# Moving the w_in operations of VectorE into the steps that form the bits, and GpSimd's split of the next pair's q ahead of its k

## The chip, the cores and the metric

One core of one Trainium2 chip runs the whole program. The metric is the device time of one execution in microseconds (us), median over the runs. The engines are called here as the profile calls them: PE (TensorE), DVE (VectorE), ACT (ScalarE), POOL (GpSimd) and SP (SyncE, which only issues DMAs here); PEld is the loading of PE's weights.

## What is computed

The reference is an attention whose mask comes from a hash, and then two feed-forward layers:

```python
def _attn_ref(q, k, v, proj):
    q_bits = (np.einsum('bhsd,dk->bhsk', q, proj) > 0).astype(np.int64)
    k_bits = (np.einsum('bhsd,dk->bhsk', k, proj) > 0).astype(np.int64)
    q_bucket, k_bucket = (np.sum(x * 2 ** np.arange(6), axis=-1) for x in (q_bits, k_bits))
    mask = q_bucket[:, :, :, None] == k_bucket[:, :, None, :]
    scores = np.where(mask, scale * np.matmul(q, k.transpose(0, 1, 3, 2)), -1e9)
    attn = np.exp(scores - np.max(scores, axis=-1, keepdims=True))
    attn = attn / (np.sum(attn, axis=-1, keepdims=True) + 1e-09)
    return np.matmul(attn, v)
def _moe_ref(x, w_in, w_out):
    h = np.maximum(x @ w_in, 0.0)
    return h * h @ w_out
def _moe2_ref(x, w_in, w_out):
    h = x @ w_in
    return h * (1.0 / (1.0 + np.exp(-h))) @ w_out
```

There are 2 batches of 8 heads, 768 positions of 64 dimensions; the layers take 1536 rows of 512 and widen them to 2048. All is float32; the kernel forms its products from two parts, a rounded high one and the rest.

## The kernel before

The 16 heads form eight pairs, p = 0 to 7. A pair is four units u (a head and one half of its 768 query rows), and a unit is three score tiles of 128 query rows by 768 keys. One loop, `for d in range(-5, ...)`, writes out the instructions of attention by hand: pass d, called **step d** here, issues on each engine a fixed list, and since each engine runs its queue in order, this order is the schedule. A step takes

- on DVE: the negated row maximum of the score tile of the step before (L983, `row_max`), the low part `tl` of the odd transposed block of the step before (L1023, `t_lo`), two tiny operations on the maximum (L987 and L988), then whatever the list `mid[d]` holds, then `tl` of the even block of this step;
- on PE: the transposes of two blocks of the probabilities (L1012, three matmuls each) into tiles `t`, the products with v of two earlier blocks (L1036 with the high part `th`, L1037 with `tl`), and the next score tile `s` (L976, four matmuls);
- on ACT: `th`, the rounded copy of each block (L1017), and the exponential of the score tile (L996);
- on POOL and SP: what the list `todo[d]` holds, at the end of the step.

The tiles `t` share three PSUM buffers in turn, so a block's transposes wait until the block three places earlier has been read by its `t_lo`.

In **a bits step** (d = 1, 10, 22, 34, 46, 58 and 70, the table `long`) PE also forms the hash products of a coming pair, eight matmuls with 32 columns of weights each, into a tile `bs` that takes one of the three buffers as well (L786, `bits_mm`). DVE therefore does the odd block's `t_lo` in the bits step already, right behind the even one, and in the next step compares `bs` with zero (L791, `bits_cmp`). ACT scales the pair's q after the hash products (L758).

In **a turn step** (d = 17, 29, 41, 53, 65, 77 and 88, the table `turn`) PE makes one more small transpose (L1251) and ACT copies its result.

The weights arrive as 64-bit floats in two 32-bit words, and the first layers' tiles are turned to float32 during attention. The table `W_STEPS` (line 41) holds for each of the four first w_in tiles the steps of its load, of |x| on ACT with the limits on POOL (L937, L941), and of three operations on DVE, which stand in `mid`: `w_exp` (L945, shifts), `w_sign` (L949) and `w_low` (L953), each on 128 x 512 words in SBUF. The last two read two SBUF tiles. `wp_put` (L960, L961, POOL) then rounds and splits the finished tile, for the first two.

Per pair POOL also rounds k and q (`cast_pair`, L754) into `hk` and `hq`, subtracts (`split_pair`, L774) into `lp`, splits v (`split_v`, L919 and L920), sums the outputs (`x_sum`, L1082) and starts one DMA per head for the high part of k (L764). For the second pair on, with d0 = 12(p - 1) and the bits step at d0 - 2, q and k are loaded by SP at d0 - 10 and d0 - 9, split around the bits step, and go to the score operands `qq` and `kk` by SP's DMAs: `hq` (L766), `lp` (L779 and L780, `place_lo`) and the bits (L909, `place_bits`). The first scores of the pair are issued at step d0 + 7.

Behind attention the two layers run by an order that a planner makes from costs at build time; the change doesn't touch it.

Of the kernel before, what the change touches and what calls it, by code (L numbers as in the profile page):

```python
# [37 lines left out]
W_LO = float(np.uint32(897 << 20).view(np.float32))  # L38
W_HI = float(np.uint32((1150 << 20) | 0xFFFFF).view(np.float32))
V_LAG = 4  # L40
W_STEPS = ((0, 5, 17, 29, 53), (8, 17, 41, 65, 77), (22, 29, 41, 92, 93), (54, 65, 92, 96, 96))
WA = 4
FB = 4
NP = FB // 2
# [655 lines left out]
def lsh_attention_moe_moe(ctx, tc, kd, qk, qf, fq, v, pc, wi1, wo1, wi2, wo2, out):  # L700
# [408 lines left out]
    def at(g, fn, *a):  # L1109
        todo[g].append((fn, a))  # L1110

    for p in range(1, NPAIR):
        d0 = 12 * (p - 1)
        if p > 1:
            at(d0 - 10, load_pair, p)
            at(d0 - 9, load_k, p)
            at(d0 - 4, new_hi, p)
            at(d0 - 4, cast_pair, p, 1)
            at(d0 - 3, split_pair, p, 1)
            scale[d0 - 2] = p  # L1120
            at(d0 - 2, cast_pair, p, 0)
            at(d0 - 1, split_pair, p, 0)
        else:
            at(0, split_pair, p, 0)
            at(0, split_pair, p, 1)
        long[max(d0 - 2, 1)] = p
        at(d0 + 1, load_head, p, 0)
        at(d0 + 2, place_lo, p, 0)
        at(d0 + 2, place_bits, p, 0)
        at(d0 + 5, load_v, p)  # L1130
        at(d0 + 8, split_v, p)
        at(d0 + 7, load_head, p, 1)
        at(d0 + 8, place_lo, p, 1)
        at(d0 + 8, place_bits, p, 1)
    for p in range(NPAIR):
        d0 = 12 * (p + 1)
# [12 lines left out]
    for k, d in enumerate(X_STEPS):  # L1149
        at(d, x_form, k)  # L1150
    for i, (d_load, d_abs, *d_dve) in enumerate(W_STEPS):
        key = (0, 0, i)
        at(d_load, w_load, key)
        at(d_abs, w_abs, key)
        at(d_abs, w_limit, key)
        for d, fn in zip(d_dve, (w_exp, w_sign, w_low)):
            mid[d].append((fn, (key,)))
        d0 = d_dve[2]
        if i < 2:
            at(d0, wp_put, i)  # L1160
    early = [(0, 1, i) for i in range(WB)]
    for i, key in enumerate(early):
        at(82 + 12 * i, w_load, key)
# [1 line left out]
    with tc.manual_schedule():  # L1165
# [106 lines left out]
        p = NPAIR - 1  # L1272
# [73 lines left out]
```

## Time and profile before

| what | value |
|---|---|
| time, median of 3 runs | 715.39 us (715.32 to 716.03) |
| the profiled execution's own time | 717.23 us |
| its span, first to last instruction | 715.5 us |
| busy: PE, DVE, ACT, POOL | 707.4 (99%), 605.4 (85%), 537.7 (75%), 257.6 us (36%) |
| DVE in the first thirteen of 40 slices | 90% or more in nearly all |
| granted TensorE clock | full (1.000 as a mean, the 2.4 GHz level) |

The profile is of one execution. Its times count from the first instruction; a row of the order of time gives the start, the duration, the engine, the line of the program, the operation with what it writes and reads, and in brackets how long the engine sat idle before it and what it waited for. Instructions on one engine overlap: the next may start some 0.1 us before the end that is shown for the one ahead. Attention takes the first 223 us or so, the two layers the rest.

### The profile page before, as it was taken

The numbers are of one execution on the slowest core, as the hardware profiler recorded it, in microseconds if no ns is written. First come the engines' busy times: TensorE is split into PE (matmuls) and PEld (weight loads), VectorE is DVE, ScalarE is ACT, GpSimd is POOL, SyncE is SP. The second block draws the span as 40 slices with busy tenths as digits, with TensorE's granted clock in tenths as the row PEclk, the third lists the DMA queues.
The fourth block names the chain that finished last, engine by engine and source line by source line (L and its number), as shares of the span: only waits on it lengthen the run. The fifth ranks groups of instructions, "written<-read, shape, count | busy, mean of one in ns | idle before, by whom it ended". The sixth has DMA issues, their size and how long they took to land.

```text
span 715.5 us, 10860 instructions
## 1 busy us (share of the span) xinstructions
PE 707.4 (99%) x3610; PEld 602.9 (84%) x3610; DVE 605.4 (85%) x1099; ACT 537.7 (75%) x1012; POOL 257.6 (36%) x239
## 2 busy tenths in 40 slices
PE   9999999999999999999999999999999999999998
PEld 4899999999998888888887888888888888888886
DVE  6999999999999879887897789988878778888840
ACT  6999999999997787594477469788765955854861
POOL 7546575657665221042231241245114011212300
PEclk9999999999999999999999999999999999999999
DMA  5778967967733455242534832487221332245432
GB/s 171 206 177 194 228 159 193 232 160 198 174 96 86 110 162 118 89 131 46 117 89 122 183 93 73 104 184 174 71 73 60 101 106 86 76 103 119 103 110 96
DMA packets 39495, 92.51 MB, mean 129 GB/s; under 512 B 5944, under 2 KB 11588, under 8 KB 39440
## 3 DMA queue, kind: packets, MB, share of 16 engines
q1 hardware_dynamic: 26976, 67.58, 31.6%
q0 software_dynamic: 12032, 23.79, 18.7%
q8 instruction: 28, 0.46, 0.3%
q10 hardware_dynamic: 432, 0.46, 0.2%
q14 instruction: 27, 0.22, 0.1%
HBM read 52.32 MB, written 3.19 MB: 78 GB/s over the span
## 4 chain that ended last, share of the span: by engine, by line
PE 87%; DVE 10%; issue 1%; DMA 1%; ACT 0%; DVEq 0%; ACTq 0%; POOLq 0%
PE bank L558 36%; PE bank L443 24%; PE bank L420 7%; PE s L976 6%; PE t L1012 6%; DVE mt L983 4%; DVE tl L1023 4%; PE o L1036 3%; PE o L1037 3%; DMA cell<-cell 1%; PE bs L786 1%; PE warm L967 1%; DVE mt L988 1%; DVE mt L987 0%; ACT P L996 0%
## 5 line engine op out<-in xcount | busy, mean ns | idle before, releaser
L558 PE MATMUL bank<-woh,cell 128*128 128x512 f32 (+1 forms) x392 | 119.8, 385 | 0.0
L558 PE MATMUL bank<-cell,woh 128*128 128x512 f32 x384 | 118.4, 389 | 1.1 <-DMA cell<-cell 1.1
L996 ACT ACTIVATE P<-s,mt 128x768 f32<-128x768 f32 x96 | 95.6, 995 | 13.5 <-DVE mt L988 11.7
L1023 DVE TENSOR_TENSOR tl<-t,th 128x384 fp32r<-128x384 f32 x192 | 104.0, 547 | 0.1
L983 DVE TENSOR_REDUCE mt<-s 128x1 f32<-128x768 f32 x96 | 91.3, 951 | 3.1 <-PE s L976 2.4
L558 PEld LDWEIGHTS bank<-cell,woh 128*128 128x128 f32 x384 | 72.1, 188 | 16.4 <-DMA cell<-cell 1.5
L558 PEld LDWEIGHTS bank<-woh,cell 128*128 128x128 f32 x392 | 73.1, 188 | 14.6
L1017 ACT CAST th<-t 128x384 fp32r<-128x384 f32 x192 | 82.2, 482 | 3.2 <-PE t L1012 3.0
L976 PE MATMUL s<-kk,qq 76*128 76x384 f32 (+1 forms) x384 | 83.4, 338 | 0.5 <-ACT P L996 0.3
L1012 PE MATMUL t<-ident,P 128*128 128x128 f32 x576 | 80.6, 273 | 1.8 <-DVE tl L1023 1.8
L1012 PEld LDWEIGHTS t<-ident,P 128*128 128x128 f32 x576 | 67.5, 140 | 11.3 <-DVE tl L1023 7.2
L278 DVE TENSOR_TENSOR cell<-bank,cell 128x512 f32<-128x512 f32 x91 | 62.1, 691 | 17.5 <-PE bank L443 13.1
L443 PE MATMUL bank<-xw,wpb 128*128 128x512 f32 x312 | 75.9, 389 | 0.0
L558 PE MATMUL bank<-wol,cell 128*128 128x512 f32 (+1 forms) x196 | 75.4, 385 | 0.0
L558 PE MATMUL bank<-cell,wol 128*128 128x512 f32 x192 | 74.7, 389 | 0.0
L1036 PE MATMUL o<-th,vv 128*128 128x384 f32 x192 | 72.7, 379 | 0.0
L976 PEld LDWEIGHTS s<-kk,qq 76*128 76x128 f32 (+1 forms) x384 | 67.9, 188 | 2.3 <-ACT P L996 1.6
L443 PEld LDWEIGHTS bank<-xw,wpb 128*128 128x128 f32 x312 | 58.5, 188 | 12.4 <-DVE bank L278 0.3
L1037 PE MATMUL o<-tl,vv 128*128 128x384 f32 x192 | 64.7, 337 | 0.0
L450 ACT COPY cell<-bank 128x512 f32<-128x512 f32 x39 | 22.9, 586 | 39.5 <-PE bank L443 37.5
L268 ACT CAST cell<-cell 128x512 fp32r<-128x512 f32 x81 | 48.8, 617 | 2.8 <-DMA cell<-cell 1.7
L271 POOL DMA_DIRECT2D cell<-cell x23 | 20.5, 906 | 82.4 <-ACT cell L270 59.4
(185 smaller groups left out, 1461.2 us busy)
## 6 DMA issues: line engine op xcount, KB each, us to landing
raw<-in_dram SPq DMA_DIRECT2D x62, 512.0 KB
cell<-cell POOLq DMA_DIRECT2D x23, 256.0 KB, 3.8
qq<-hq SPq DMA_DIRECT2D x28, 192.0 KB
kk<-in_dram POOLq DMA_DIRECT2D x14, 384.0 KB, 4.5
yf<-cell POOLq DMA_DIRECT2D x21, 256.0 KB, 3.6
vr<-in_dram SPq DMA_DIRECT2D x8, 384.0 KB
ta<-ob SPq DMA_DIRECT2D x31, 96.0 KB
tb<-ob SPq DMA_DIRECT2D x31, 96.0 KB
```

What stands on the lines that cost most here:

```text
L278: add("DVE", 0.70, lambda: vec.tensor_tensor(out=val(out), in0=bank[b], in1=val(other), op=ALU.add), [("bank", b), *reads], writes)
L420: mm(bank[b], wpa[n][:, p, 4 * h + j], x[:, q], start=j == 0 and z == 0, stop=j == 3 and z == 2)
L443: mm(bank[b], w[:, p], x[:, q], start=not started and z == 0, stop=z == 2, skip_group_check=started)
L558: mm(bank[b][:, 0:wd], x, y, start=start and i == 0 and z == 0, stop=i == (FB if half is None else 2 * half + 2) - 1 and z == 2, skip_grou ...
L976: mm(s[:, n, 0:QW], t["qq"][h][0:kk, ab, c0 : c0 + 128], t["kk"][h][0:kk, ab, n * QW : (n + 1) * QW], start=ab == 0, stop=ab == 1)
L983: nc.vector.tensor_reduce(out=m[:, 0:1], in_=s[:, :, 0:QW], op=ALU.max, axis=AX.XY, negate=True)
L996: nc.scalar.activation(out=e.rearrange("p (a b) -> p a b", a=2), in_=s[:, :, 0:QW], func=AF.Exp, scale=m[:, 1:2], bias=m[:, 2:3], accum_ou ...
L1012: nc.tensor.transpose(t[:, j * 128 : (j + 1) * 128], P[u, j][:, kt * 128 : (kt + 1) * 128], ident)
L1017: nc.scalar.copy(out=th, in_=PT[g][0][:, 0:QW])
L1023: nc.vector.tensor_tensor(out=tl, in0=t[:, 0:QW], in1=th.bitcast(F32), op=ALU.subtract)
L1036: mm(o[:, 0:QW], vv, th, start=kt == 0, stop=False)
L1037: mm(o[:, 0:QW], vv, tl, start=False, stop=kt == KT - 1)
```

## The change

Three things change, all in the tables that place work in steps. The operations of DVE on the w_in tiles leave steps 17, 29, 41, 53, 65 and 77 for 10, 22, 34, 46, 58 and 70: tile 0's three to 10, 22, 34; tile 1's to 46, 58, 70; tile 2's first to 46 (its others stay at 92 and 93, and tile 3's where they were). `wp_put` follows seven steps behind the last of them, at 41 and 77 (53 and 77 before). For each pair from the third on (p = 2 to 7) POOL rounds and splits q first and then k, all four put at the bits step, where k stood at two and one steps before it and q at it and one behind. `place_lo` of a pair's first head moves from d0 + 2 to d0 + 3, and so behind the load of the next pair's q.

```diff
-W_STEPS = ((0, 5, 17, 29, 53), (8, 17, 41, 65, 77), (22, 29, 41, 92, 93), (54, 65, 92, 96, 96))
+W_STEPS = ((0, 5, 10, 22, 34), (8, 17, 46, 58, 70), (22, 29, 46, 92, 93), (54, 65, 92, 96, 96))
...
-            at(d0 - 4, new_hi, p)
-            at(d0 - 4, cast_pair, p, 1)
-            at(d0 - 3, split_pair, p, 1)
             scale[d0 - 2] = p
-            at(d0 - 2, cast_pair, p, 0)
-            at(d0 - 1, split_pair, p, 0)
+            at(d0 - 2, new_hi, p)
+            for i in range(2):
+                at(d0 - 2, cast_pair, p, i)
+                at(d0 - 2, split_pair, p, i)
...
-        at(d0 + 2, place_lo, p, 0)
+        at(d0 + 3, place_lo, p, 0)
         at(d0 + 2, place_bits, p, 0)
...
-            at(d0, wp_put, i)
+            at(d0 + 7, wp_put, i)
```

DVE in step 22, a bits step, and in step 23. Before (`mt` is the row maximum, `tl` the low part of a block, `bn` the compared bits):

```order
L983 TENSOR_REDUCE mt<-s_2_1055 128x1
L1023 TENSOR_TENSOR tl_1064<-t_1043,th_1047 128x384
L987 TENSOR_SCALAR mt<-mt 128x1
L988 TENSOR_SCALAR mt<-mt 128x1
L1023 TENSOR_TENSOR tl_1074<-t_1068,th_1072 128x384
L1023 TENSOR_TENSOR tl_1090<-t_1076,th_1080 128x384
L983 TENSOR_REDUCE mt<-s_0_1094 128x1
L987 TENSOR_SCALAR mt<-mt 128x1
L988 TENSOR_SCALAR mt<-mt 128x1
L791 TENSOR_SCALAR bn_1110<-bs_1099,tmt 128x384
L1023 TENSOR_TENSOR tl_1118<-t_1112,th_1116 128x384
```

And now:

```order
L983 TENSOR_REDUCE mt<-s_2_1052 128x1
L1023 TENSOR_TENSOR tl_1059<-t_1040,th_1044 128x384
L987 TENSOR_SCALAR mt<-mt 128x1
L988 TENSOR_SCALAR mt<-mt 128x1
L949 SCALAR_TENSOR_TENSOR wi_288<-rx,wi_288 128x512
L1023 TENSOR_TENSOR tl_1070<-t_1064,th_1068 128x384
L1023 TENSOR_TENSOR tl_1086<-t_1072,th_1076 128x384
L983 TENSOR_REDUCE mt<-s_0_1090 128x1
L987 TENSOR_SCALAR mt<-mt 128x1
L988 TENSOR_SCALAR mt<-mt 128x1
L791 TENSOR_SCALAR bn_1112<-bs_1095,tmt 128x384
L1023 TENSOR_TENSOR tl_1120<-t_1114,th_1118 128x384
```

`w_sign` of tile 0 (L949), which stood in step 29, now stands ahead of the two low parts of step 22.

POOL around the same bits step, from the split of v on (`vv`) to the load of the next pair's high part of k. Before:

```order
L920 TENSOR_TENSOR vv_908<-vr_909,vv_908 128x12x64
L754 CAST hk_1025<-rk_802 128x768
L774 TENSOR_TENSOR lp_1060<-rk_802,hk_1025 128x768
L1054 TENSOR_SCALAR sums_566<-sums_566 128x12
L754 CAST hq_1024<-rq_801 128x768
L774 TENSOR_TENSOR lp_1060<-rq_801,hq_1024 128x768
L764 DMA kk_0_1204<-in_dram 64x2x768
```

And now:

```order
L920 TENSOR_TENSOR vv_908<-vr_909,vv_908 128x12x64
L1054 TENSOR_SCALAR sums_566<-sums_566 128x12
L754 CAST hq_1101<-rq_800 128x768
L774 TENSOR_TENSOR lp_1104<-rq_800,hq_1101 128x768
L754 CAST hk_1102<-rk_801 128x768
L774 TENSOR_TENSOR lp_1104<-rk_801,hk_1102 128x768
L764 DMA kk_0_1205<-in_dram 64x2x768
```

k's two operations (`hk`, and `lp` from `rk`) went from ahead of q's to behind them.

SP for the first head of the pair that follows. Before:

```order
L779 DMA qq_0_1203<-lp_1060 64x768
L780 DMA kk_0_1204<-lp_1060 64x768
L909 DMA qq_0_1203<-bn_1110 12x384 x2
L909 DMA kk_0_1204<-bn_1110 12x384 x2
L741 DMA rq_1246<-in_dram 128x768
L744 DMA rk_1247<-in_dram 128x768
```

And now:

```order
L909 DMA qq_0_1204<-bn_1112 12x384 x2
L909 DMA kk_0_1205<-bn_1112 12x384 x2
L741 DMA rq_1245<-in_dram 128x768
L779 DMA qq_0_1204<-lp_1104 64x768
L780 DMA kk_0_1205<-lp_1104 64x768
L744 DMA rk_1246<-in_dram 128x768
```

The two DMAs of the low parts went behind the four of the bits and the load of the next q.

## Rows read from the trace of the kernel before

**Rows 1.** The page's chain of work that ended last: share of the span by engine.
```profile
PE 87%; DVE 10%; issue 1%; DMA 1%; ACT 0%; DVEq 0%; ACTq 0%; POOLq 0%
```

**Rows 2.** Score matmuls on PE in order of time: start us, duration, engine, line, operation.
```profile
54.38 0.86 PE L976 MATMUL s<-kk,qq 128*128 128x384 f32 x4
56.66 0.86 PE L976 MATMUL s<-kk,qq 128*128 128x384 f32 x4
...
80.34 0.86 PE L976 MATMUL s<-kk,qq 128*128 128x384 f32 x4
83.24 0.86 PE L976 MATMUL s<-kk,qq 128*128 128x384 f32 x4
85.30 0.86 PE L976 MATMUL s<-kk,qq 128*128 128x384 f32 x4
...
106.93 0.86 PE L976 MATMUL s<-kk,qq 128*128 128x384 f32 x4
109.55 0.86 PE L976 MATMUL s<-kk,qq 128*128 128x384 f32 x4
...
133.24 0.86 PE L976 MATMUL s<-kk,qq 128*128 128x384 f32 x4
135.79 0.86 PE L976 MATMUL s<-kk,qq 128*128 128x384 f32 x4
...
185.72 0.86 PE L976 MATMUL s<-kk,qq 128*128 128x384 f32 x4
188.28 0.86 PE L976 MATMUL s<-kk,qq 128*128 128x384 f32 x4
```

**Rows 3.** DVE in order of time, steps 17 and 53, at the w_in operations.
```profile
54.64 0.42 DVE L945 TENSOR_SCALAR wi<-wi 128x512 uint32<-128x512 uint32 x1
54.97 0.55 DVE L1023 TENSOR_TENSOR tl<-t,th 128x384 fp32r<-128x384 f32 x1
...
133.49 0.68 DVE L953 SCALAR_TENSOR_TENSOR wi<-rx,wi 128x512 uint32<-128x512 uint32 x1
134.09 0.55 DVE L1023 TENSOR_TENSOR tl<-t,th 128x384 fp32r<-128x384 f32 x1
```

**Rows 4.** PE in order of time: the transposes of step 54.
```profile
133.93 0.49 PE L1012 MATMUL t<-ident,P 128*128 128x128 f32 x3
134.70 0.55 PE L1012 MATMUL t<-ident,P 128*128 128x128 f32 x3 [0.27 <-DVE tl L1023]
```

**Rows 5.** DVE in order of time: step 29's w_in operation.
```profile
80.60 1.03 DVE L949 SCALAR_TENSOR_TENSOR wi<-rx,wi 128x512 uint32<-128x512 uint32 x1
```

**Rows 6.** POOL in order of time: around bits step 22, and step 29.
```profile
62.30 1.84 POOL L920 TENSOR_TENSOR vv<-vr,vv 128x768 fp32r<-128x768 f32 x1
...
64.99 1.83 POOL L774 TENSOR_TENSOR lp<-rk,hk 128x768 fp32r<-128x768 f32 x1
...
67.52 0.82 POOL L754 CAST hq<-rq 128x768 fp32r<-128x768 f32 x1 [0.41 <-ACT rq L758]
...
79.25 1.84 POOL L1082 TENSOR_TENSOR ta<-ta,tb 128x768 f32<-128x768 f32 x1 [3.16 <-DMA tb<-ob]
```

**Rows 7.** DVE in order of time: bits step 22, step 23 and the start of 24.
```profile
65.25 1.01 DVE L1023 TENSOR_TENSOR tl<-t,th 128x384 fp32r<-128x384 f32 x2
...
67.44 0.68 DVE L791 TENSOR_SCALAR bn<-bs,tmt 128x384 fp32r<-128x384 f32 x1
68.03 0.55 DVE L1023 TENSOR_TENSOR tl<-t,th 128x384 fp32r<-128x384 f32 x1
68.79 0.96 DVE L983 TENSOR_REDUCE mt<-s 128x1 f32<-128x768 f32 x1 [0.21 <-PE s L976]
```

**Rows 8.** PE in order of time: the transposes of steps 23 and 24.
```profile
66.46 0.87 PE L1012 MATMUL t<-ident,P 128*128 128x128 f32 x6
...
68.59 0.82 PE L1012 MATMUL t<-ident,P 128*128 128x128 f32 x6
```

**Rows 9.** SP in order of time: the last issues for the pair first scored at 85.30.
```profile
79.36 1.47 SPq L909 DMA_DIRECT2D kk<-bn  x2
80.87 0.51 SPq L741 DMA_DIRECT2D rq<-in_dram  x1
81.44 0.42 SPq L744 DMA_DIRECT2D rk<-in_dram  x1
```

## The prediction

> **What bounds the kernel now.** I read the chain of waits first. PE holds 87% of it and DVE 10% [rows 1]: most of the time only less work on PE would help, but in places DVE sets the pace. Where those places are, the order of time on PE shows. From one score tile to the next, a plain step takes 2.06 us (83.24 to 85.30) [rows 2]. Behind the six turn steps that hold w_in operations it is more: 2.28 at step 17 (54.38 to 56.66), 2.90 at 29, 2.62 at 41, and 2.55 at 53, 65 and 77, of which the first and last stand there [rows 2]. The excess over 2.06 is 0.22 + 0.84 + 0.56 + 3 x 0.49 = 3.09 us. That is all that this part of the change can win, 0.43% of the time.
>
> Why a w_in operation costs time on PE is seen at step 53. `w_low` holds DVE from 133.49 to 134.09, when the low part behind it starts: 0.60 us, of the 0.68 shown for it [rows 3]. That low part ends at 134.09 + 0.55 = 134.64, and PE, which needs its PSUM buffer, goes on at 134.70 after 0.27 us idle [rows 4], so 0.06 after DVE's end. The three transposes behind the wait take 0.55 where those without one take 0.49 [rows 4]: another 0.06 is lost at a wait. `w_exp` is shorter, 54.64 to 54.97, 0.33 us [rows 3].
>
> Step 29 is dearer for another reason. `w_sign` took 1.03 us there [rows 5], 0.35 more than its like at step 53. POOL's `x_sum` ran from 79.25 to 81.09 [rows 6], and the DVE operation, started at 80.60, ended at 81.63, 0.54 behind POOL: it looks as if it did its work only when POOL was done. The Trainium skill's page "SBUF — State Buffer", section "Who interferes with whom", says the same of a DVE instruction with two SBUF inputs and a GpSimd instruction that reads SBUF: one holds the shared port for its whole length, the other waits. This trace agrees, with the 0.54.
>
> **The change part by part.** No instruction is added or removed; 3.09 us go, and the question is what the same operations cost in the bits steps.
>
> *The bits step.* Eight hash matmuls make PE's step longer, so DVE has something to spare. Rows of step 22 to 24 show how much. The new operation stands right behind the row maximum's two small ones, so the two low parts that start at 65.25 [rows 7], and all behind them, start later by its length x. Three waits of PE then matter, each 0.06 behind DVE's end:
> - The odd block of step 23 needs the second low part, which ends at 66.26 [rows 7]. Six transposes take 0.87 from 66.46 on [rows 8] where three take 0.49 [rows 4], so the odd block's three start 0.38 later, at 66.84. Spare: 66.84 - 66.26 - 0.06 = 0.52.
> - The even block of step 24, at 68.59 [rows 8], needs the buffer of the hash products, read until 67.44 + 0.68 = 68.12 [rows 7]. Spare: 0.41.
> - The odd block of step 24 needs the low part that ends at 68.03 + 0.55 = 68.58 [rows 7]. By the same count (0.82 for six [rows 8] less 0.49) it starts 0.33 after 68.59, at 68.92. Spare: 0.28.
>
> DVE's own idle time there, 0.21 us ahead of the maximum at 68.79 [rows 7], says much the same. The three delays do not add up, as DVE is late by the same x each time; the smallest spare decides. An operation costs x - 0.28, and 0.06 for the wait: 0.38 for x = 0.60, 0.11 for 0.33, and 0.45 for the two `w_exp` together (x = 0.67). After that PE is late by more than DVE and nothing waits again.
>
> *The sum.* Steps 22, 34, 58 and 70 hold one long operation each, 4 x 0.38 = 1.52; step 10 one short, 0.11; step 46 two, 0.45. Together 2.08, against 3.09 before: **1.01 us are won**. Of this 0.35 is the meeting with POOL that goes, and the rest some 0.1 us per operation, as a turn step spares about 0.17 us of DVE (0.60 - 0.49 + 0.06) and a bits step 0.28.
>
> The bounds: an operation in a bits step can cost nothing (all covered), which wins 3.09; it can't win more, as the hash products stay. Or nothing is covered and each costs its length and 0.06: 0.33 + 4 x 0.60 + 0.67 + 6 x 0.06 = 3.76, which loses 0.67. I take 2.08, as its spares come from the very steps into which the operations go.
>
> *What stays in the turn steps.* The copy of a w_in tile on ACT at 17, 29 and 65 loses the DVE stall that ran beside it. I cost this at nothing: the low part that it delays has the turn step's extra transpose on PE as cover. Without that cover it could show some 0.1 us at each of three steps.
>
> *POOL.* q's split waits for ACT's scaling, as its rounding at 67.52 shows [rows 6], and then q and k follow in one piece. k's split now ends some 2.7 us later than q's did (one rounding of 0.82 and one split of 1.83 [rows 6]). Behind it on POOL's queue stand the load of the next pair's k, then the work on the outputs; at this pair `x_sum` waited 3.16 us for a DMA [rows 6], which swallows the delay. What it buys: k's split ran from 64.99 to 66.82 [rows 6], just where the w_in operation will now stand (from 65.25). It is out of the way, and v's split is over at 64.14 [rows 6], 1.11 us earlier. `wp_put` at 41 in place of 53 costs nothing: the two layers, long after, read its result.
>
> *SP.* The low parts' two DMAs go behind the bits' four and the load of q. They will be issued about where the load of k stands now, until 81.44 + 0.42 = 81.86 [rows 9], and the first scores that read them come at 85.30 [rows 2], or some 0.6 us earlier after the change (0.22 + 0.84 won by then, 0.11 + 0.38 paid). About 2.8 us are left for the transfer. Nothing queued behind them waits longer for POOL: k's low part is ready at 67.52 + 2 x (0.82 + 1.83), at 72.8 [rows 6].
>
> The layers behind attention keep their order and should start 1.0 us earlier. The profiled execution took 717.23 us, 1.84 more than the median of 715.39. 717.23 - 1.01 = 716.2 in a like execution, and **714.4 us** as a median. About 0.2% (1.43 us) is what a measurement of this kernel can tell from no change, so I expect "same", on the good side.
>
> **The rivals.**
> 1. *The bits step covers nearly all.* For it: the hash products are work that only PE has, and my three spares are read at one bits step alone. Against it: DVE's second low part and the compare stand in the same two steps and leave but 0.21 us idle [rows 7]. From 0.30 per long operation downwards it passes 0.2%: 713.9 down to 715.39 - 3.09 = 712.3. Chance 0.16.
> 2. *Nothing is covered.* The two low parts behind the operation are both needed by PE's next transposes, so the whole length shows, and the stall only moves. Up to 715.39 + 0.67 = 716.1. For it: where PE waits now it is for exactly these [rows 4]; against it: the 0.52 and 0.41 above. Chance 0.10.
> 3. *The operations meet POOL in the bits steps.* Place: DVE from 65.25 on, POOL's split of v. If that split runs over 1.11 us later than now (its data come by SP's DMA, which stands behind `x_sum`), a w_in operation waits for its end, up to the 1.84 us of a split [rows 6]. With half of it lost at each of the six bits steps that is 6 x 0.92 = 5.5 us, less the 1.01: 719.9, and slower. By the page of the Trainium skill named above it is the same: had k's split stayed first, its rule would stop the operation in every bits step. Against it: v's split ends 1.1 us or more ahead at this pair, and nothing that feeds it moves before its DMA is issued. Chance 0.06.
> 4. *The low parts come late.* If their transfer took over 2.8 us behind the 384 KB of q, PE would wait at the first scores of six pairs; one us over makes 6 - 1 = 5 us, 720.4. Against it: the DMA of the bits had 4.5 us to spare (80.83 to 85.30) [rows 9]. Chance 0.05.
>
> **How the numbers follow.** The forecast has 0.63, rival 1 0.16, 2 0.10, 3 and 4 together 0.11. Faster by over 0.2%: rival 1 and the lucky edge of the forecast, 0.19. Slower by over 0.2%: rivals 3 and 4, less mild forms of them, 0.09. Same: 0.72. The range must leave out no more than 0.2: from 713.3, which cuts the far part of rival 1, to 715.8, which takes most of rival 2 and cuts 3 and 4. The forecast's own range is 713.9 to 715.0 (0.5 either way: 0.1 us for each of five long operations).
>
> **What would show it.** Right: PE's step behind 17, 29, 41, 53, 65 and 77 is the plain 2.06; the steps around 22, 34, 58 and 70 are longer by 0.3 to 0.45 together, with PE's transposes of step 24 waiting for DVE's low part; every `w_sign` and `w_low` up to step 70 takes 0.68. Wrong: bits steps without any new wait of PE (rival 1), 0.6 us each (rival 2), a w_in operation of over 1 us in a bits step (rival 3), or PE waiting for a DMA ahead of a pair's first scores (rival 4).

## The result, and the profile after

The changed kernel takes **720.59 us** as a median of 4 runs (719.39 to 721.09), the kernel before on the same chip 715.66 (715.32 to 716.03). The ratio is 1.0067, with a 95% interval of 1.0054 to 1.0080: slower by 0.7%, outside the range of 713.3 to 715.8, and on the side that had 0.09. The profiled execution took 720.13 us, its span is 718.0.

The view to start from is the order of time of the score matmuls on PE, as for [rows 2]. Here are the score tiles of steps 17 and 18, 29 to 31 and 41 to 43 of the changed kernel. A step is counted, as in the prediction, from the start of its own score tile to the start of the next one's.

```profile
54.19 0.86 PE L976 MATMUL s<-kk,qq 128*128 128x384 f32 x4
56.24 0.88 PE L976 MATMUL s<-kk,qq 128*128 128x384 f32 x4
...
80.49 0.86 PE L976 MATMUL s<-kk,qq 128*128 128x384 f32 x4
82.55 0.86 PE L976 MATMUL s<-kk,qq 128*128 128x384 f32 x4
85.82 0.94 PE L976 MATMUL s<-kk,qq 128*128 128x384 f32 x4 [1.04 <-DMA rk<-in_dram]
...
109.31 0.86 PE L976 MATMUL s<-kk,qq 128*128 128x384 f32 x4
111.36 0.88 PE L976 MATMUL s<-kk,qq 128*128 128x384 f32 x4
113.98 0.94 PE L976 MATMUL s<-kk,qq 128*128 128x384 f32 x4 [0.39 <-DMA kk<-lp]
```

The turn steps do what was foretold: 17, 29 and 41 take 2.05, 2.06 and 2.05 us (54.19 to 56.24, 80.49 to 82.55, 109.31 to 111.36), where [rows 2] has 2.28, 2.90 and 2.62. But right behind the turn steps 29 and 41 stands something new: 3.27 us (82.55 to 85.82) and 2.62 us (111.36 to 113.98) in place of 2.06. These are the first scores of pairs 3 and 4, and PE waits there for a DMA. The first wait is put down to `rk`, which no score reads; PE's operands are `qq` and `kk`, and the DMA of theirs next to `rk` on SP is the low part `kk<-lp`. So the first wait is taken for one on `kk<-lp` too, which the second wait names outright.

DVE and POOL at bits step 34 show the other loss. DVE, then POOL:

```profile
92.43 2.04 DVE L953 SCALAR_TENSOR_TENSOR wi<-rx,wi 128x512 uint32<-128x512 uint32 x1
94.39 1.01 DVE L1023 TENSOR_TENSOR tl<-t,th 128x384 fp32r<-128x384 f32 x2
```
```profile
91.18 0.82 POOL L919 CAST vv<-vr 128x768 fp32r<-128x768 f32 x1 [6.01 <-DMA vr<-in_dram]
92.09 1.84 POOL L920 TENSOR_TENSOR vv<-vr,vv 128x768 fp32r<-128x768 f32 x1
```

`w_low` takes 2.04 us where it took 0.68 [rows 3]. It ends at 94.47, 0.54 behind the end of POOL's split of v at 93.93: the meeting of [rows 5, 6], with the same 0.54. Shorter meetings with v's split stand at steps 22, 46 and 70 (`w_sign` 0.76, the first `w_exp` 0.99, `w_low` 0.82). v's split is late because v's load is: POOL sat idle for 6.01 us in front of its rounding. Before, the load of the same v was issued by SP, and v was rounded and split by POOL, at

```profile
83.19 0.57 SPq L915 DMA_DIRECT2D vr<-in_dram  x1
```
```profile
87.74 0.82 POOL L919 CAST vv<-vr 128x768 fp32r<-128x768 f32 x1 [2.64 <-DMA vr<-in_dram]
88.64 1.84 POOL L920 TENSOR_TENSOR vv<-vr,vv 128x768 fp32r<-128x768 f32 x1
```

Over the eight pairs this idle time is, in the list of what POOL's line 919 waited for, before

```profile
  DMA vr<-in_dram: 11.4, 5
```

and after (us, times)

```profile
  DMA vr<-in_dram: 29.4, 7
```

The chain of work that ended last, by engine (a q behind a name is the engine's issuing of work), where [rows 1] had DVE at 10% and DMA at 1%:

```profile
PE 86%; DMA 5%; DVE 4%; POOL 2%; SPq 2%; issue 1%; ACT 1%; POOLq 0%; DVEq 0%; ACTq 0%
```

DVE's share fell as planned, and DMA, POOL and SP came onto the path. Two pieces of that chain, with start and duration from the issue on, are the two transfers:

```profile
83.89 7.23 DMA vr<-in_dram
...
108.75 5.09 DMA kk<-lp
```

Why both are late stands on SP. For the pair first scored at 85.82, against [rows 9]:

```profile
77.73 2.21 SPq L909 DMA_DIRECT2D kk<-bn  x2
80.05 0.46 SPq L741 DMA_DIRECT2D rq<-in_dram  x1
80.56 0.52 SPq L779 DMA_DIRECT2D qq<-lp  x1
81.17 0.54 SPq L780 DMA_DIRECT2D kk<-lp  x1
81.76 0.58 SPq L744 DMA_DIRECT2D rk<-in_dram  x1
82.44 0.76 SPq L1049 DMA_DIRECT2D ta<-ob  x1
83.30 0.54 SPq L1049 DMA_DIRECT2D tb<-ob  x1
83.89 0.58 SPq L915 DMA_DIRECT2D vr<-in_dram  x1
```

The two low parts, 192 KB each, now stand between the loads of q and k, 384 KB each, and v's 384 KB wait behind all of them. The view by stretches shows what that does to the DMA engines; the columns are the stretch in us and its length, the busy time of PE, PEld, DVE, ACT and POOL, the granted clock, and at the end the busy share of the DMA engines (which this view gives over 1 in full stretches) and GB/s. Before:

```profile
76.00:78.00 2.00, 2.00 (x15) 1.95 (x14) 2.00 (x6) 1.77 (x5) 0.09 (x1) 1.00 1.10 238
78.00:80.00 2.00, 2.00 (x16) 1.94 (x16) 2.00 (x6) 2.00 (x6) 0.75 (x1) 1.00 0.82 204
80.00:82.00 2.00, 1.53 (x10) 1.25 (x9) 2.00 (x6) 1.99 (x6) 1.08 (x1) 1.00 0.21 57
```

After:

```profile
76.00:78.00 2.00, 2.00 (x16) 1.96 (x15) 2.00 (x6) 1.77 (x5) 1.53 (x2) 1.00 1.07 247
78.00:80.00 2.00, 2.00 (x16) 1.94 (x15) 2.00 (x6) 2.00 (x6) 1.51 (x1) 1.00 0.16 33
80.00:82.00 2.00, 2.00 (x15) 1.96 (x14) 1.91 (x6) 2.00 (x6) 0.00 (x0) 1.00 0.45 104
```

Before, the low parts (issued at 75.35 and 76.22) were carried ahead of the loads of q, k and v. Now the engines have little to do from 78 to 82, at 33 and 104 GB/s, and the low parts fall into the full stretch behind it. From 78 to 87 us all 758 DMA packets of the changed kernel are of the one hardware queue that carries SP's transfers, so no other queue's bytes stood in their way there.

All steps of attention, sorted by kind, for every kernel of this study (the difference to the profiled execution before, in us, from the starts of the score matmuls; "turn" is steps 17, 29, 41, 53, 65 and 77, "bits" the bits steps with the step behind each, "first" the two steps at a pair's first scores, 18, 19, 30, 31 and so on; what is left is about 0.1 or less, and the parts are good to some 0.04; the ratio and its interval are estimated from the single runs and need not be the quotient of the two medians: three runs of e8 took 717.85 to 721.26):

| kernel | turn | bits | first | attention | median, us | ratio, 95% interval |
|---|---|---|---|---|---|---|
| forecast | -3.09 | +2.08 | 0 | -1.01 | 714.4 | |
| changed kernel | -3.12 | +4.35 | +2.64 | +3.97 | 720.59 | 1.0067 [1.0054, 1.0080] |
| e1_lo_back | -3.12 | +2.14 | +0.02 | -0.92 | 715.47 | 0.9994 [0.9985, 1.0004] |
| e2_lo_late | -0.34 | +0.01 | +0.74 | +0.38 | 716.85 | 1.0017 [1.0007, 1.0027] |
| e3_pool_order | +0.42 | 0.00 | +0.01 | +0.38 | 716.58 | 1.0013 [1.0004, 1.0022] |
| e4_w_steps | -3.12 | +5.77 | +0.03 | +2.69 | 720.29 | 1.0069 [1.0051, 1.0088] |
| e5_lo_late_w_steps | -3.12 | +4.50 | +3.22 | +4.66 | 723.08 | 1.0106 [1.0091, 1.0120] |
| e6_lo_late_pool | +0.13 | 0.00 | +0.60 | +0.71 | 717.31 | 1.0024 [1.0014, 1.0034] |
| e7_v_first | -3.12 | +1.83 | +0.02 | -1.26 | 714.73 | 0.9990 [0.9981, 0.9999] |
| e8_loads_behind | -3.12 | +2.21 | +0.04 | -0.89 | 715.25 | 1.0007 [0.9991, 1.0022] |
| e9_v_and_q_ahead | -3.12 | +2.21 | +9.34 | +8.45 | 725.16 | 1.0136 [1.0112, 1.0161] |
| e10_v_first_again | -3.12 | +1.81 | +0.04 | -1.26 | 715.32 | 0.9994 [0.9983, 1.0004] |

So the time came from two places: 4.35 us in bits steps where 2.08 were foretold, and 2.64 us at first scores where nothing was. The kernel before had a median of 715.66 in the runs beside the changed kernel and e1 to e4, 715.70 beside e5 to e8 and 715.82 beside e9 and e10.

### The profile page after: what moved, and what is told of

Same layout as the page of the kernel before. It is cut to its first block, busy times and chain, and to the rows that moved or that the text cites. A ratio compares the mean times of both kernels' runs of the same rounds, so it can differ in the third digit from the quotient of the medians.

```text
span 718.0 us, 10867 instructions
## 1 busy us (share of the span) xinstructions
PE 709.2 (99%) x3609; PEld 602.1 (84%) x3610; DVE 608.1 (85%) x1099; ACT 538.8 (75%) x1012; POOL 258.3 (36%) x239
## 4 chain that ended last, share of the span: by engine, by line
PE 86%; DMA 5%; DVE 4%; POOL 2%; SPq 2%; issue 1%; ACT 1%; POOLq 0%; DVEq 0%; ACTq 0%
PE bank L558 36%; PE bank L443 25%; PE bank L420 7%; PE s L976 6%; PE t L1012 5%; PE o L1036 3%; PE o L1037 3%; DVE mt L983 2%; DMA rx<-in_dram 1%; DMA qq<-hq 1%; DVE tl L1023 1%; DMA vr<-in_dram 1%; PE warm L967 1%; SPq L909 1%; DMA kk<-lp 1%
## 5 line engine op out<-in xcount | busy, mean ns | idle before, releaser
L588 ACT COPY yf<-bank 128x512 f32<-128x512 f32 x48 | 27.9, 585 | 31.5 <-PE bank L558 29.5
```

## The experiments

The change has three parts: the w_in operations in bits steps, POOL's order, and the late low parts. The first four runs undo one part or make one part alone. The theory is that the late low parts crowd SP's DMA queue at both places (A); its rivals blame POOL's order (B) or the bits steps with the w_in operations in themselves (C).

**e1_lo_back: the changed kernel, with the low parts' DMAs where they were.**

```diff
-        at(d0 + 3, place_lo, p, 0)
+        at(d0 + 2, place_lo, p, 0)
```

> The change with one part undone: the low parts' two DMAs of a pair's first head stand on SP at d0 + 2 again, ahead of the bits' four. Theory A (these two DMAs' place is the cause: in the changed kernel PE's first scores of a pair came late in steps 30, 42 and 66 by 1.21 + 0.56 + 0.44, and v's DMA, in the same crowd, landed so late that POOL's split of v met the w_in operations of steps 34 and 46): both go, the bits steps cost what I predicted or slightly more (0.38 to 0.45 per long operation), 714.4 to 715.2 us. Theory B (POOL's new order is the cause, as k's low part is ready 2.7 us later): still 718 to 721. Theory C (the bits steps themselves are dear): the first scores are on time, but the steps 34 and 46 stay 1.0 to 1.8 us too long, 717 to 718.5.

Measured: 715.47 us, ratio 0.9994 [0.9985, 1.0004]. This one line takes away 5.1 us, though the median lies 0.3 above A's numbers. Both losses go together: first scores are on time (+0.02), and POOL's wait for v falls from 29.4 to

```profile
  DMA vr<-in_dram: 18.0, 7
```

with the bits steps at +2.14, where the forecast had 2.08. At step 46 alone the step and its next are 0.70 longer instead of 0.45: one `w_exp` there still met v's split and took 0.73 us where its like took 0.42. So the low parts' place in SP's order set v's time too, though neither reads the other.

**e2_lo_late: the kernel before, with the late low parts alone.**

```diff
-        at(d0 + 2, place_lo, p, 0)
+        at(d0 + 3, place_lo, p, 0)
```

> The kernel before with only this part of the change: the low parts' DMAs of the first head at d0 + 3, behind the bits and the load of the next q. Theory A: PE waits at the first scores of the pairs, 2 to 3 us in all, and v's DMA lands late but no w_in operation stands where v is split: 717.5 to 719. Theory B: 715.7, the same as before, since k's low part is ready early in POOL's old order. Theory C: 715.7.

Measured: 716.85 us, 1.0017 [1.0007, 1.0027]; attention +0.38. This is under A's numbers and over those of B and C. At steps 18 and 19 PE is 0.74 late, at the other pairs' first scores not at all; a meeting of `w_sign` with `x_sum` at step 29 [rows 5, 6] was missed by luck, which gives 0.35 back. So the one line that costs 5.1 us in the changed kernel costs 1.2 in the kernel before. Something else of the change multiplies it.

**e3_pool_order: the kernel before, with POOL's new order alone** (the part of the diff on `cast_pair` and `split_pair`).

> The kernel before with only POOL's new order (q rounded and split ahead of k, all behind v's split, low parts' DMAs in their old place). Theory A: nothing waits, 715.4 to 716. Theory B: k's low part, ready 2.7 us later, reaches the scores late: 717 to 719. Theory C: 715.7.

Measured: 716.58 us, 1.0013 [1.0004, 1.0022], attention +0.38. This is over A's numbers by 0.6 and under B's by 0.4. First scores and bits steps are as before; the 0.4 us is one w_in operation, at turn step 77 (3.01 for 2.55): `w_low`, at 185.79, took 1.15 us for 0.68 beside POOL's `x_sum` from 184.54 to 186.38. POOL's order alone costs little and gains nothing while the operations stand in turn steps.

**e4_w_steps: the kernel before, with the w_in operations moved alone.**

```diff
-W_STEPS = ((0, 5, 17, 29, 53), (8, 17, 41, 65, 77), (22, 29, 41, 92, 93), (54, 65, 92, 96, 96))
+W_STEPS = ((0, 5, 10, 22, 34), (8, 17, 46, 58, 70), (22, 29, 46, 92, 93), (54, 65, 92, 96, 96))
...
-            at(d0, wp_put, i)
+            at(d0 + 7, wp_put, i)
```

> The kernel before with only the w_in operations (and wp_put) moved, POOL's old order and SP's old places. Theory A with the collision that the prediction named: k's split (64.99 to 66.82 at step 22 before) stands where the w_in operation now stands, so each long one takes some 2.0 us in place of 0.68 and costs 1.7 to 1.9: 719 to 723. If POOL does not hold DVE up: 714.5 to 715. Theory C: 717 to 719 without long w_in operations.

Measured: 720.29 us, 1.0069 [1.0051, 1.0088]. First scores on time, bits steps +5.77: steps 46, 58 and 70 with the step behind cost 1.80, 1.68 and 1.47. The time is within the numbers of the collision, which came at three of the six steps. DVE there, and POOL:

```profile
65.31 0.72 DVE L949 SCALAR_TENSOR_TENSOR wi<-rx,wi 128x512 uint32<-128x512 uint32 x1
...
117.59 1.83 DVE L945 TENSOR_SCALAR wi<-wi 128x512 uint32<-128x512 uint32 x1
...
145.14 2.04 DVE L949 SCALAR_TENSOR_TENSOR wi<-raw,wi 128x512 uint32<-128x512 uint32 x1
```
```profile
65.41 1.29 POOL L754 CAST hk<-rk 128x768 fp32r<-128x768 f32 x1
...
117.31 1.83 POOL L774 TENSOR_TENSOR lp<-rk,hk 128x768 fp32r<-128x768 f32 x1
...
144.81 1.83 POOL L774 TENSOR_TENSOR lp<-rk,hk 128x768 fp32r<-128x768 f32 x1
```

At steps 46 and 58 the operation starts 0.28 and 0.33 behind k's split and lasts until 0.28 and 0.54 behind its end. At step 22 DVE was first by 0.10 us, and POOL's rounding had to wait instead (1.29 us for 0.82). So POOL's new order is needed for the moved operations: with it the three steps cost 0.70, 0.32 and 0.38 (e1).

Left open was what makes the late low parts dear: POOL's order, with k's split last (B), or PE itself, which comes earlier to the first scores once the turn steps hold no operation (A). The next two runs add to the late low parts one of the other two parts each.

**e5_lo_late_w_steps: the kernel before, with the late low parts and the moved operations; POOL as before** (e2 and e4 together).

> The kernel before with the late low parts (place_lo at d0 + 3) and the moved w_in operations; POOL keeps k ahead of q. The w_in operations alone, in POOL's old order, gave 720.29 and +2.69 us in attention; the late low parts alone +0.38. Theory A (the low parts queue behind the 384 KB of q on SP, and what they cost is set by how early PE comes to the first scores, which is 0.3 to 0.85 us earlier once the turn steps hold no w_in operation): first scores late by 1.5 to 2.7 us over all pairs as in the changed kernel, step 30 by over 1 us, attention +4.2 to +5.4, about 721.5 to 723. Rival B (it takes POOL's new order, with k's split last, to make the low parts late): first scores late by no more than in the run with the late low parts alone (0.7), attention +3.1, about 720.7. The bits steps 46, 58 and 70 stay near 4.5 in both.

Measured: 723.08 us, 1.0106 [1.0091, 1.0120]. First scores +3.22, where B allowed 0.7 and A said 1.5 to 2.7: A's side and beyond, without POOL's order. Attention +4.66 is inside A's numbers, and the median 0.1 above its time. The profiled run took 720.12 us and the three others 722.95 to 723.64, so some 3 us of the median are not in this trace. The step late by over 1 us is not 30, as A had it, but 18, with 3.18 us:

```profile
55.90 0.88 PE L976 MATMUL s<-kk,qq 128*128 128x384 f32 x4
59.09 0.94 PE L976 MATMUL s<-kk,qq 128*128 128x384 f32 x4 [0.95 <-DMA rk<-in_dram]
```

The bits steps 58 and 70 did not stay near 4.5, as both theories said, but fell to 3.29 and 3.56. The operations met less of k's split here and more of v's, which is late as in the changed kernel (POOL waited 25.2 us in all for v). At step 70 `w_low` ran from 174.30 to 175.43 and v's split from 173.03 to 174.87; at 22, 34 and 46 an operation met v's split as well.

**e6_lo_late_pool: the kernel before, with the late low parts and POOL's new order; operations in the turn steps.**

> The kernel before with the late low parts and POOL's new order; the w_in operations stay in the turn steps. Theory A (lateness counts only once PE is early, so it takes the moved w_in operations): first scores late by about 0.7 in all, as with the late low parts alone, attention +0.4 to +0.8, 716.5 to 717.2. Rival B (POOL's order makes them late): step 30 late by about 1 us, first scores 2 to 2.7, attention +2 to +2.7 and 718 to 718.5. In both v's split should end later than before, without a price, as no w_in operation stands in a bits step.

Measured: 717.31 us, 1.0024 [1.0014, 1.0034]. First scores +0.60 and attention +0.71, which is A (the median lies 0.1 above A's range). POOL's wait for v rises to

```profile
  DMA vr<-in_dram: 19.1, 6
```

and costs nothing, as no w_in operation stands in a bits step. B falls.

The runs that follow change only the places of DMAs in SP's order.

**e7_v_first: the changed kernel, low parts back, and v's load ahead of the next pair's q and k.**

```diff
-            at(d0 - 10, load_pair, p)
-            at(d0 - 9, load_k, p)
+            at(d0 - 8, load_pair, p)
+            at(d0 - 7, load_k, p)
...
-        at(d0 + 3, place_lo, p, 0)
+        at(d0 + 2, place_lo, p, 0)
...
-        at(d0 + 5, load_v, p)
+        at(d0 + 2, load_v, p)
```

> The changed kernel with the low parts back at d0 + 2 and v's load ahead of the next pair's q and k (v at d0 + 2, q and k at d0 + 4 and d0 + 5 of the pair ahead). Theory A (what is issued first on SP's queue lands first, so v's split is over well ahead of the bits step): no w_in operation meets v's split; step 46 falls from 3.49 to about 3.15 and w_exp there from 0.99 to 0.42; attention 1.2 to 1.3 us under before's, about 714.3 to 715.0. Rival (the meeting at 46 is with another operation of POOL, or v waits for something else than its place in the queue): step 46 stays at 3.5, about 715.5 as with the low parts back alone. If q and k come late in turn, the scaling on ACT and the hash products in the bits steps wait for a DMA, and it is slower than 715.5.

Measured: 714.73 us, 0.9990 [0.9981, 0.9999]; attention -1.26. POOL's wait for v is down to 1.3 us, and every operation on w_in tiles up to step 70 has the length that [rows 3] show:

```profile
L949 DVE SCALAR_TENSOR_TENSOR wi<-rx,wi x1: 682/682/682, 65.2 to 65.2; 128x512 uint32<-128x512 uint32 x1
L949 DVE SCALAR_TENSOR_TENSOR wi<-raw,wi x1: 683/683/683, 143.5 to 143.5; 128x512 uint32<-128x512 uint32 x1
```
```profile
L953 DVE SCALAR_TENSOR_TENSOR wi<-rx,wi x1: 683/683/683, 91.3 to 91.3; 128x512 uint32<-128x512 uint32 x1
L953 DVE SCALAR_TENSOR_TENSOR wi<-raw,wi x1: 680/680/680, 169.6 to 169.6; 128x512 uint32<-128x512 uint32 x1
```

(The columns are the shortest, median and longest in ns, and the first and last start.) Step 46 fell from 3.49 (e1) to 3.18. This is the bits step without any meeting, and so the forecast's own case.

**e8_loads_behind: the changed kernel, its late low parts kept, but the next q and k loaded behind v.**

```diff
-            at(d0 - 10, load_pair, p)
-            at(d0 - 9, load_k, p)
+            at(d0 - 7, load_pair, p)
+            at(d0 - 6, load_k, p)
```

> The changed kernel, its late low parts kept at d0 + 3, but the next pair's q and k loaded three steps later, behind v. Theory A (crowding on SP's queue: low parts behind q's 384 KB, v behind all of them): first scores on time (2.06 to 2.08 at steps 30, 31, 42, 43, 66), v's split over before the bits steps, so bits steps 22, 34, 58, 70 near 3.12 and 46 near 3.15 to 3.5; attention 0.9 to 1.3 us under before's, about 714.3 to 715.5. Rival (the low parts are late because of their own later issue, at d0 + 3 instead of d0 + 2, or because k's split is last on POOL, whatever stands ahead of them on SP): first scores still late by about 2.7 us, attention at or over +1, 717 or more.

Measured: 715.25 us, 1.0007 [0.9991, 1.0022]; attention -0.89. SP for the same pair as above:

```profile
77.40 1.48 SPq L909 DMA_DIRECT2D kk<-bn  x2
78.99 0.52 SPq L779 DMA_DIRECT2D qq<-lp  x1
79.61 0.54 SPq L780 DMA_DIRECT2D kk<-lp  x1
80.25 0.53 SPq L1049 DMA_DIRECT2D ta<-ob  x1
80.88 0.56 SPq L1049 DMA_DIRECT2D tb<-ob  x1
81.48 0.58 SPq L915 DMA_DIRECT2D vr<-in_dram  x1
82.12 0.43 SPq L741 DMA_DIRECT2D rq<-in_dram  x1
```

The low parts are still issued at d0 + 3, behind the bits, but with no 384 KB ahead of them. First scores are on time (+0.04), and POOL waits 3.2 us in all for v. So neither the step of their issue nor k's split makes them late by itself. This run alone doesn't part the bytes ahead from 1.6 us of earlier issue (79.61 for 81.17); e9 does.

**e9_v_and_q_ahead: the changed kernel, with v's load ahead of q's and of the late low parts.**

```diff
-        at(d0 + 5, load_v, p)
+        at(d0 + 2, load_v, p)
```

> The changed kernel with one move: v's load goes from d0 + 5 to d0 + 2, ahead of the next q's load and of the late low parts (d0 + 3). So 768 KB stand ahead of the low parts on SP's queue where 384 KB did, and v comes first. Theory A (what lands late is what stands behind other bytes on the queue; this trace moves about 290 to 310 GB/s in its busy stretches, so 384 KB more are an estimated 1.3 us): POOL's wait for v falls from 29.4 us to a few; bits steps as with v first (about 1.8 us over before in all); first scores late by about 1.3 us more at each of six pairs, 8 to 10.5 us in all where it was 2.7; attention 6 to 9 us over before, 722 to 725. Rival (the low parts are late by their own issue, one step later, not by the bytes ahead): first scores late by 2.7 us as in the changed kernel, bits steps 1.8, attention +1.4, about 717.

Measured: 725.16 us, 1.0136 [1.0112, 1.0161]; first scores +9.34 and attention +8.45, both in theory A's numbers; bits steps +2.21 where it had about 1.8, and the median 0.2 above its range. PE's waits in attention (in all, times, longest), and the first scores of the same pair as above:

```profile
PE s L976 <- DMA kk<-lp: 6.4, 4, 2.5
```
```profile
83.17 0.86 PE L976 MATMUL s<-kk,qq 128*128 128x384 f32 x4
...
87.16 0.94 PE L976 MATMUL s<-kk,qq 128*128 128x384 f32 x4 [1.76 <-DMA kk<-lp]
```

Here `kk<-lp` was issued at 81.35, 0.18 later than in the changed kernel, and PE went on at 87.16 instead of 85.82, 1.34 later. The other 1.2 us are put down to the 384 KB more ahead of it (1.3 was the estimate). This run also parts the two losses: v is early and every operation on w_in tiles in a bits step has its plain length, while the low parts are later than ever. What no run tried is the low parts on another queue, so it stays open whether they would wait there too, for the DMA engines that the queues share.

**e10_v_first_again: the kernel of e7 once more.**

> The same kernel as the one with v first, for a second interval. Theory A: 0.998 to 0.9995 of the time before, that is faster, though by no more than 0.2%; attention 1.2 to 1.3 us under before's. Rival (its first 0.9990 was luck of the chip): 1.000 or more.

Measured: 715.32 us against 715.82, 0.9994 [0.9983, 1.0004]; attention -1.26 again. The interval holds 1 and the theory's numbers alike. The trace's gain is there both times, and the time's is some 0.05 to 0.1%. Against the changed kernel it is 5 us; against the kernel before it is at the edge of what can be told.

## Why the prediction was wrong

By its own steps:

- **Turn steps: right.** 3.09 us were to go, 3.12 went in every run with the moved operations, down to the plain 2.06.
- **The bits step's price: right, where the operations stand alone.** The spare of 0.28 us, read at one bits step, gave 0.38 per long operation, 0.11 at step 10 and 0.45 at 46, together 2.08. e7 shows 0.39, 0.32, 0.32 and 0.39 for the long ones, 0.03 and 0.38 for the others, together 1.83. Rivals 1 (covered) and 2 (nothing covered) fall.
- **"About 2.8 us are left for the transfer" and so no cost: the first step that failed.** The gap was foretold well: the issue of `kk<-lp` ended at 81.71, and by a plain step PE would have come to it at 84.61 (82.55 + 2.06), 2.90 us later. But PE went on at 85.82, 4.11 us behind the end of the issue, and the 1.21 between the two is what step 30 lost. For the next pair it took 4.69 (from 109.29 to 113.98). The prediction had put the transfer's cost at nothing and set against the 2.8 only the bits' DMAs with 4.5 us to spare, which carry 18 KB each. A row for a large transfer behind other loads was there unread: before, the issue of v's 384 KB ended at 83.76 and POOL's rounding of v started at 87.74, 3.98 us later. It would have said that 2.8 may not do.
- **The gain spent its own cover.** Before, a turn step's excess right ahead of the first scores also gave the transfers time. In the changed kernel step 41 wins 0.57 and step 42 loses 0.56; 65 wins 0.50 and 66 loses 0.44; 29 wins 0.84 and 30 loses 1.21. The prediction did count PE's earlier arrival (0.6 us), but against a transfer time that it had not measured. e5 and e6 show the pairing: late low parts cost 3.22 at first scores with the moved operations and 0.60 without.
- **"Nothing that feeds it [v's split] moves before its DMA is issued": the second step that failed.** v's DMA was issued 0.70 us later than before (83.89 for 83.19), but its split started 3.45 later (92.09 for 88.64). The low parts had moved into the stretch in which v's load is carried. The margin of 1.11 us at step 22 was read at one pair; at step 34 v's split ended at 93.93, 1.50 us into the w_in operation, a cost that the sum had at nothing.
- **Rivals 3 and 4 together are what happened.** They were priced at 5.5 and 6 us before the gain of 1.01 was taken off; the meetings cost 4.35 - 1.83 = 2.5, the late low parts 2.64. They were given 0.11 together and treated as two accidents. They have one cause, the place of 384 KB on SP's queue, and e1 takes nearly all of both away with one line (first scores +0.02, bits steps +2.14).
- **POOL's order: right as a reason.** Without it k's split stops the operation at steps 46, 58 and 70 (e4). With it, and v early, nothing meets.
- **The layers behind attention: not settled.** Attention tells -1.26 in e7 and the median -0.97 and -0.50; it tells +3.97 in the changed kernel and the median +4.93. The runs that were only timed leave no record of steps, so whether attention or the layers vary there, also in e5, stays open. The profiled execution before was itself 1.84 us above its median, with a wait of 1.1 us of PE for a DMA in the layers.

The forecast's -1.01 was thus a good account of DVE and PE, and no account of SP's queue. With only `place_lo` left where it was, the time was 715.47 (e1), inside the stated range.

## What to carry to other kernels

In these runs a DMA that was moved behind a large load on the same queue paid for the bytes ahead of it, and what was queued behind it paid for its own bytes. So read the landing time of the nearest transfer of like size from the trace before you call a gap enough. Look too at where the DMA engines stand idle, since a transfer that leaves an idle stretch for a full one can delay what is carried there, as it did v here. And when a stall goes, ask what had been landing under it; here two turn steps gave their gain back within the next step.

## What the hardware showed that was not expected

- The meeting with POOL also stops `w_exp`, an operation with one SBUF input: 1.83 us for 0.42 in e4 (117.59), 0.99 in the changed kernel at step 46. What the prediction read from its rows was a two-input operation. The Trainium skill, page "SBUF — State Buffer", section "Who interferes with whom", lists `tensor_scalar` among the operations that can take the shared ports too, when their operands meet the conditions of a two-port mode; the trace agrees, with the 1.83.
- In these rows it goes by who starts first: DVE, ahead by 0.10 us, took 0.72 for 0.68, and POOL's rounding took 1.29 for 0.82 (e4, 65.31 and 65.41). Where POOL was ahead, DVE waited (changed kernel, 92.09 and 92.43).
- `kk<-lp`, 192 KB, needed 4.65 us from the start of its issue until PE went on behind 384 KB of q in the changed kernel, and 5.81 behind 768 KB of v and q in e9 (81.35 to 87.16), each time with the other low part's 192 KB ahead of it as well. v's 384 KB took 4.55 before and 7.23 us in the changed kernel, with the low parts' 384 KB more in front. That is 2.7 us for these 384 KB, where v's cost the low parts 1.2 in e9; why the two differ was not tried.
